# A new order table for the steps of the attention phase

## The chip, the cores and the metric

One core of a Trainium2 chip runs the whole program. The metric is the device time of one execution in microseconds (us). TensorE (PE) multiplies matrices, VectorE (DVE), ScalarE (ACT) and GpSimd (POOL) work on elements, and SyncE (SP) issues every DMA. Each engine takes its own instructions in the order in which they stand in its list; engines wait for each other through semaphores.

## The reference

Attention with a block-causal mask over 4 batches of 8 heads, 576 positions and 64 dimensions, then two mixers, all in f32 (weights of the mixers come as 64-bit floats):

```python
scores = scale * np.matmul(q, k.transpose(0, 1, 3, 2))
scores = np.where(block_i >= block_j, scores, -1000000000.0)   # blocks of 64 positions
scores = scores - np.max(scores, axis=-1, keepdims=True)
attn = np.exp(scores)
attn = attn / (np.sum(attn, axis=-1, keepdims=True) + 1e-09)
x = np.matmul(attn, v)                                         # then heads side by side: B x S x 512
u = x + (np.maximum(x.transpose(0, 2, 1) @ w_tok1, 0.0) @ w_tok2).transpose(0, 2, 1)
x = u + np.maximum(u @ w_ch1, 0.0) @ w_ch2                     # 512 -> 1536 -> 512
xn = (x - mu) / np.sqrt(var + 1e-06) * g_ln
out = x + np.maximum(xn @ w_ch1b, 0.0) @ w_ch2b                # 512 -> 2048 -> 512
```

## The kernel before

Precision is kept by splitting every operand into a high and a low part and multiplying three of the four pairs. The program has two phases.

The attention phase works on 16 pairs of heads (p = 0 to 15), eight chunks of token mixing (q = 0 to 7, two pairs each), the rebasing of the 64-bit token weights, and the first weights and rows of the MLPs. Each of these is cut into small steps, and a table of words, `ORDER`, says in which order the steps are issued. A word is a step's name and the number of its pair, chunk or tile (without a number: how often the name has come so far). There is no scheduler behind it: walking through the table fills each engine's list, so two steps of one engine run in the table's order, and a step that waits holds up all that stands behind it on that engine.

The steps of one pair, with their engines: `lqk`, `lv`, `lt` load queries and keys, values, and the last 64 positions (SP). `rlk`, `rlq` relay them (ACT, POOL). `trk`, `trq`, `trr` transpose them (PE, line 110); `kh`, `qh`, `rmh` write their high planes (ACT, line 313), `kl`, `ql`, `rml` the low ones (DVE, line 311). `s3`, `s1`, `s02`, `s4` are four groups of score matmuls (PE, lines 340, 345, 370); `m3` and so on their row maxima (DVE, lines 380, 382); `n` the negation (ACT, line 390); `e` the exponents (ACT, lines 396, 405); `h` and `l` the high and low halves of the exponents (line 425 and 429: `h3`, `h02`, `h4`, `l3`, `l1`, `l4` on POOL, `h1`, `l02` on DVE; for pair 15 `l4` is on DVE and `h1` on POOL). `tA` and `tB` are DMA transposes of those halves (SP, line 437). `a3`, `a1`, `a20`, `a4` multiply with the values (PE, lines 456, 471), whose planes are `vh` (ACT) and `vl` (DVE, line 326). `dn`, `ev`, `ev4` divide and empty the result (DVE, lines 487 and 494; ACT).

The buffers bound how far steps can run ahead: scores have two PSUM buffers, so a score group waits for the exponents of the group two before it; attention outputs have one, which `ev` (line 494) frees; three PSUM buffers serve everything else; `hlB` and `ptB`, the source and the target of `tB`, exist once, `hlA` and `ptA` twice; raw queries and keys once.

A token weight is loaded by `tl`, and rebased by `td0` (ACT), `td1` (DVE, four instructions, lines 133 to 139), `td2` (ACT), `td3` (POOL). A chunk is mixed by `xh`, `xl`, `t1a`, `t1b` (PE, line 553), `rh`, `rl`, `t2a` to `t2c` (PE, line 576), `ua` to `uc` (DVE, line 586), and stored by `us0`, `us1`. For the MLPs, `bwl` loads a weight, `bw0` to `bw3` rebase and split it (`bw1`: DVE, four instructions, lines 789 to 796), `bnl` loads a row tile (SP, line 867), `ba`, `bk`, `bh`, `bo`, `bt` scale, split and transpose it (`bo`: DVE, line 892), `b1` is the first layer of the first unit (PE, line 954).

Behind the table `Mlps.run` works through 35 units of an MLP's two layers (lines 954 and 991), with its own code and its own order.

Of the kernel before, what the change touches and what calls it, by code (L numbers as in the profile page):

```python
# [52 lines left out]
    td3:2 rlk trk td1 qh n02 kh h1 rlq e02 trr a3 trq td2:3 vl vh ql m3 tB s02 kl a20 a1 n3 s1 m02 rmh a4
    e3 vl n02 h02 l1 h4 trk rml m1 e02 td0:7 s3 lqk l02 n1 e1 td0:4 m3 tl l4 h1 rlq lv:4 s4 td0 h3 ev4 n3
    lv:3 ev m4 qh rlk n4 s1 abv ql e3 td1:4 td3:3 cmm l3 tA td1 td1 e4 abv h02 l1 tB kh kl lv m1 td2:4 n1
    s4 td2:5 abv td2 a20 l02 bwl dn a3 a1 trr tA a4 e1 s02 rmh h4 td2 m4 l4 ev s3 h1 cd1 cmm:5 h3 tB trk
    n4 ev4 rml m02 a3 l1 e4 s1 trq vh l3 a4 dn s4 m3 n02 td3:7 a1 vl e02 td3:5 h02 kh cd1:5 tA a20 cmm:4
    s02 trr:6 m1 n3 kl e3 lqk l02 h4 n1 l4 m4 xh e1 lv qh n4 h1 xl ev4 td3:4 rlq cd1:4 e4 ql trr:5 s3 vh
    rlk t1a l1 t1b vh s1 bwl:2 m02 n02 dn tB h3 vl:5 rmh:6 trq m3 ev trk h4 e02 vl:4 rmh:5 l3 bw0 n3 lqk
    rml:6 s02 dn a1 e3 rh kh m1 rlk abv rml:5 lv:8 h02 td3 a3 lv:7 rl t2b qh l4 a20 m02 l02 n1 a4 abv:8 kl  # L60
    ql ub e1 n02 tA ev t2c h3 abv:7 s4 m4 ev4 e02 cmm:8 tB uc h1 a3 trk s1 l3 rlq n4 cmm lqk l1 t2a cd1:8
    m1 xh kh cmm:6 kl s3 xl a4 n1 e4 e1 a1 h02 ua trq cd1 cd1:6 vh s02 rlq m3 vl t1a h1 a20 l02 n3 tA h4
    m02 s4 qh rlk t1b lqk e3 trq m4 ql ev4 trr n02 e02 lv vh:8 l4 n4 rh s1 e4 qh dn a1 s3 h3 rlk ev m1 l1
    rlq l3 rmh trk rl n1 trr ql rml h02 tB a3 s02 t2a e1 dn kh m3 kl rmh a4 n3 a20 vh:7 m02 l02 tA e3 lqk
    s3 rml t2c ua trq s4 m3 t2b uc m4 h4 n02 e02 trk l4 abv a1 ev4 h1 ub n3 h3 l3 qh ev bwl:1 e3 kh vl:8
    us1 us0 l1 rlq rlk s02 xh h3 n4 ql trr tB vl:7 e4 xl rmh m02 s4 trk a3 a20 m4 n02 a4 s1 h4 rml t1a e02
    kl tA n4 t1b lqk lv dn h02 trq l4 lv l3 s3 m1 n1 l02 e4 e1 kh ev rh abv kl cmm rl t2c h1 s1 ev4 l1 qh
# [1070 lines left out]
```

## Time and profile before

| | us |
|---|---|
| median of three runs | 938.29 |
| the three runs | 933.63, 938.29, 939.14 |
| the profiled execution, its own time | 932.9 |
| its span, first to last instruction | 931.1 |

| engine, over the span | busy us | instructions |
|---|---|---|
| PE | 873.0 | 5924 |
| PE weight loads | 498.5 | 5924 |
| DVE | 630.8 | 1249 |
| ACT | 346.9 | 847 |
| POOL | 215.4 | 187 |

A row of a window has its length, then busy us (and the number of instructions) of PE, PE weight loads, DVE, ACT and POOL, then the mean granted clock, the DMA share and GB/s. The shares of the whole span are an average over two phases with different limits, so stretches are read apart. In rows in order of time the first number is the start, the second the duration; brackets at a row's end give how long the engine was idle before it and what ended that. A granted clock of 1.00 is 2.4 GHz at TensorE, 0.50 is 1.2 GHz; an average between them is part of the time at either.

### The profile page before, as it was taken

What the parts mean: (1) busy time and instruction counts of PE and PEld (TensorE: products, weight loads), DVE (VectorE), ACT (ScalarE), POOL (GpSimd) and SP (SyncE); (2) the same over time, 40 slices, a digit from 0 to 9 for tenths busy, and PEclk for the clock granted to TensorE, in tenths of its full rate; (3) what the DMA queues carried; (4) which work ended last, traced back from release to release, by engine and by line L of the source; (5) the groups of instructions that cost most, each with busy time, mean ns of one, the idle gap of its engine ahead of it and who ended that gap; (6) DMA issues with size and microseconds to landing.
All of it is one profiled execution on the core that took longest, in us unless ns stands there. A gap on an engine that the chain in (4) does not pass through costs nothing.

```text
span 931.1 us, 15114 instructions
## 1 busy us (share of the span) xinstructions
PE 873.0 (94%) x5924; PEld 498.5 (54%) x5924; DVE 630.8 (68%) x1249; ACT 346.9 (37%) x847; POOL 215.4 (23%) x187
## 2 busy tenths in 40 slices
PE   6768889897889999999999989999999999999998
PEld 4657777786744454445444534455444544454444
DVE  7998889799984987678657888756555553332222
ACT  6868778886564232222212202222211221111110
POOL 4769778777000000000003434000000000000000
PEclk9679999999899999999999999999999999999999
DMA  9979999999994732221203335212011000000112
GB/s 217 223 160 207 196 206 221 180 190 196 257 235 114 202 92 91 68 68 69 68 23 69 69 90 98 93 36 68 23 46 46 23 0 1 1 1 12 57 57 79
DMA packets 193479, 96.66 MB, mean 104 GB/s; under 512 B 167744, under 2 KB 180800, under 8 KB 193408
## 3 DMA queue, kind: packets, MB, share of 16 engines
...
q14 instruction: 25, 0.20, 0.1%
...
## 4 chain that ended last, share of the span: by engine, by line
PE 43%; issue 31%; POOL 3%; DVE 2%; DMA 1%; ACT 0%; POOLq 0%
PE psy L991 21%; PE mm L954 20%; DMA ptB<-hlB 1%; POOL pl L939 1%; POOL pl L938 1%; PE mm L553 0%; POOL hlB L425 0%; POOL hlA L425 0%; POOL vr L920 0%; POOL hlB L429 0%; DVE z L931 0%; PE ps L340 0%; DVE mx L382 0%; PE mm L819 0%; DVE hlB L429 0%
## 5 line engine op out<-in xcount | busy, mean ns | idle before, releaser
L954 PE MATMUL mm<-xt,w 128*128 128x512 f16 (+1 forms) x1680 | 333.6, 358 | 4.3 <-DVE pl L892 2.9
L991 PE MATMUL psy<-w,hid 128*128 128x512 f16 x1512 | 333.8, 380 | 0.0
L954 PEld LDWEIGHTS <-w 128*128 128x128 f16 x1680 | 164.0, 98 | 167.4 <-issue 5.1
L991 PEld LDWEIGHTS <-hid 128*128 128x128 f16 x1512 | 148.2, 98 | 176.8 <-issue 1.6
L965 ACT ACTIVATE hid<-mm 128x512 f16<-128x512 f32 (+1 forms) x140 | 76.9, 552 | 381.3 <-PE mm L954 381.2
L968 DVE SCALAR_TENSOR_TENSOR hid<-mm,hid 128x512 f16<-128x512 f32 (+1 forms) x140 | 87.7, 634 | 125.0 <-ACT hid L965 125.0
L995 DVE SCALAR_TENSOR_TENSOR acc<-psy,rg,acc 128x512 f32<-128x512 f32 x72 | 53.9, 750 | 87.6 <-PE psy L991 87.6
L920 POOL TENSOR_TENSOR vr<-va,mhalf 128x4 f32<-128x4 f32 (+1 forms) x5 | 4.8, 960 | 295.8 <-DVE va L919 295.8
L340 PE MATMUL ps<-kt 64*128 64x256 f32 (+3 forms) x384 | 54.2, 400 | 18.1 <-ACT wide L405 15.2
L405 ACT ACTIVATE wide<-ps,nm 128x128 f32<-128x128 f32 (+3 forms) x128 | 65.7, 523 | 1.6
L429 POOL TENSOR_TENSOR hlA<-wide,hlA 128x1024 f16<-128x1024 f32 (+1 forms) x32 | 58.3, 1831 | 23.5 <-DVE hlA L425 15.5
L779 ACT ACTIVATE w64a<-w 128x512 f32<-128x512 f32 x56 | 37.0, 668 | 71.0 <-DVE w L859 47.7
L382 DVE TENSOR_REDUCE mx<-ps 128x2 f32<-128x768 f32 (+3 forms) x64 | 50.5, 811 | 10.7 <-PE ps L345 10.7
L995 DVE SCALAR_TENSOR_TENSOR acc<-psy,rs,acc 128x512 f32<-128x512 f32 x54 | 40.0, 748 | 26.2 <-PE psy L991 25.1
L340 PEld LDWEIGHTS ps<-kt 64*128 64x128 f32 x384 | 35.8, 223 | 26.7 <-ACT wide L405 18.9
L796 DVE SCALAR_TENSOR_TENSOR w64a<-w,w64a 128x512 int32<-128x512 int32 x56 | 40.4, 722 | 1.9
L794 DVE SCALAR_TENSOR_TENSOR w64a<-w,w64a 128x512 int32<-128x512 int32 x56 | 39.4, 703 | 1.9
L553 PE MATMUL mm<-xr,wt 128*128 128x256 f32 (+1 forms) x240 | 37.6, 307 | 0.4 <-DVE kt L311 0.4
L789 DVE TENSOR_SCALAR_CACHE_REDUCE w64a<-w64a 128x512 f32<-128x512 f32 x56 | 37.8, 674 | 0.2
L576 PE MATMUL mm<-h,wt 128*128 128x256 f32 (+1 forms) x240 | 33.1, 288 | 2.0 <-DVE kt L311 0.7
L110 PE MATMUL ptr<-ident,sc 128*128 128x128 f32 x128 | 24.0, 323 | 11.7 <-DVE kt L311 6.1
L553 PEld LDWEIGHTS mm<-xr,wt 128*128 128x128 f32 (+1 forms) x240 | 32.7, 203 | 3.7 <-PE x L471 0.5
(128 smaller groups left out, 934.5 us busy)
## 6 DMA issues: line engine op xcount, KB each, us to landing
...
```

Of the source, the lines that this page charges most:

```text
L340: nc.tensor.matmul(views[hh], kt[r, a, KQ + t * P : KQ + (t + 1) * P], kt[r, c, KK : KK + n], start=i == 0, stop=False)
L382: nc.vector.tensor_reduce(s["mx"][:, c : c + 2], ps, axis=AX.X, op=ALU.max)
L405: nc.scalar.activation(d[:, g, sl], s["ps", key][:, g, sl], AF.Exp, scale=SCALE, bias=s["nm"][:, c + g : c + g + 1], accum_out=s["rs"][:, ...
L429: (nc.vector if last else on("l" + key)).tensor_tensor(lo_, src, hi, ALU.subtract)
L553: nc.tensor.matmul(s["ps1"][:, m], w1[:r, t, a, m * P : (m + 1) * P], s["xr"][:r, c, t], start=i == 0, stop=i == 3 * NT - 1)
L794: nc.vector.scalar_tensor_tensor(ai, raw[:, :, 1], -0x40000000, ai, ALU.bitwise_and, ALU.bitwise_or)
L796: nc.vector.scalar_tensor_tensor(ai, raw[:, :, 0], 29, ai, ALU.logical_shift_right, ALU.bitwise_or)
L954: self.nc.tensor.matmul(ps.rearrange("p (t n) -> p t n", n=P), W[:, a, h * P : (h + 1) * P], self.xt[b][:, :, 4 * c + k], start=i == 0, st ...
L965: self.nc.scalar.activation(hid[:, 0, :w], ps, AF.Relu)
L968: self.nc.vector.scalar_tensor_tensor(hid[:, 1, :w], ps, 0.0, hid[:, 0, :w], ALU.max, ALU.subtract)
L991: self.nc.tensor.matmul(y, self.hid[v, h][:, a, k * P : (k + 1) * P], W[:, c], start=i == 0, stop=i == 11)
L995: self.nc.vector.scalar_tensor_tensor(self.acc[j], y, self.ps["r", v][k], self.acc[j], ALU.mult, ALU.add)
```

## The change

Only the table `ORDER` is different. It was made anew, over several sets of step durations and several phases of TensorE's clock, where the table before was made over one. Every word of the old table is in the new one, at another place; nothing else in the program differs. Its first and last rows:

```diff
 ORDER = """
-    lqk rlk tl:1 lv rlq tl:0 trk td0:1 lt td1:1 tl lqk trq kh qh td0:0 kl tl:6 tl:3 ql rlq abv s3 s1 td0
...
-    bk bs bs:8 bs
+    lqk tl:1 rlk tl:6 rlq trk td0:1 lv lv:2 td0:6 td1:1 kh trq qh lqk tl:0 kl td2:1 ql s3 m3 abv lt s1 m1
...
+    bwl bs
 """
```

VectorE, about a fifth into the attention phase, before: the last instruction of one rebase of a token weight (lines 133 to 139), two whole rebases, then a low plane of keys and, as the last row, the maximum `m1` of pair 3.

```order
L139 SCALAR_TENSOR_TENSOR w64a<-w_488,w64a 64x256
L133 TENSOR_SCALAR w64a<-w64a 128x512
L135 TENSOR_SCALAR w64a<-w64a 128x512
L137 SCALAR_TENSOR_TENSOR w64a<-w_426,w64a 128x512
L139 SCALAR_TENSOR_TENSOR w64a<-w_426,w64a 128x512
L133 TENSOR_SCALAR w64a<-w64a 128x64
L135 TENSOR_SCALAR w64a<-w64a 128x64
L137 SCALAR_TENSOR_TENSOR w64a<-w_698,w64a 128x64
L139 SCALAR_TENSOR_TENSOR w64a<-w_698,w64a 128x64
L311 TENSOR_TENSOR kt<-ptr,kt 128x512
L382 TENSOR_REDUCE mx<-ps 128x2
```

The same place after (the first rebase lacks its first instruction here); the maximum `m1` of pair 3 is the row behind two rebases:

```order
L135 TENSOR_SCALAR w64a<-w64a 128x512
L137 SCALAR_TENSOR_TENSOR w64a<-w_483,w64a 128x512
L139 SCALAR_TENSOR_TENSOR w64a<-w_483,w64a 128x512
L133 TENSOR_SCALAR w64a<-w64a 64x256
L135 TENSOR_SCALAR w64a<-w64a 64x256
L137 SCALAR_TENSOR_TENSOR w64a<-w_412,w64a 64x256
L139 SCALAR_TENSOR_TENSOR w64a<-w_412,w64a 64x256
L382 TENSOR_REDUCE mx<-ps 128x2
L429 TENSOR_TENSOR hlB<-wide,hlB 128x1024
L311 TENSOR_TENSOR kt<-ptr,kt 128x512
L380 TENSOR_REDUCE mx<-ps 128x1
```

One rebase (the 128x64 one) and the low plane of keys have moved behind this maximum; two rebases still stand ahead of it.

SyncE, near the end of the attention phase, before: from `tA` of pair 14 (first row) to `tB` of pair 15 (last row).

```order
L437 DMA_TRANSPOSE ptA<-hlA 128x24x128
L867 DMA acc_3998<-u_dram 128x512
L437 DMA_TRANSPOSE ptB<-hlB 128x26x128
L867 DMA acc_4029<-u_dram 128x512
L598 DMA u_dram<-u 64x256
L867 DMA acc_4051<-u_dram 128x512
L867 DMA acc_4085<-u_dram 128x512
L115 DMA w_4118<-in_moe_w_ch_dram 128x1024
L437 DMA_TRANSPOSE ptA<-hlA 128x24x128
L437 DMA_TRANSPOSE ptB<-hlB 128x26x128
```

And after, from the last row loads ahead of `tA` of pair 14 to `tB` of pair 15:

```order
L115 DMA w_3937<-in_moe_w_ch_dram 128x1024
L867 DMA acc_3940<-u_dram 128x512
L867 DMA acc_3967<-u_dram 128x512
L867 DMA acc_4013<-u_dram 128x512
L437 DMA_TRANSPOSE ptA<-hlA 128x24x128
L437 DMA_TRANSPOSE ptB<-hlB 128x26x128
L437 DMA_TRANSPOSE ptA<-hlA 128x24x128
L598 DMA u_dram<-u 64x256
L437 DMA_TRANSPOSE ptB<-hlB 128x26x128
```

The row loads (line 867) and the weight load (line 115) stand ahead of both transposes of pair 14; between `tB` of pair 14 and `tA` of pair 15 nothing is left, and one store (line 598) stands ahead of the last `tB`.

VectorE at the same time, before: a set of row scales, a weight rebase (line 789 to 796), two low planes of rows (line 892), and `ev` of pair 14 (line 494). Ahead of these rows stand another rebase and the two instructions of line 429 of pair 15.

```order
L826 TENSOR_SCALAR a4t<-nrm 128x4
L827 TENSOR_SCALAR a4i<-a4t 128x4
L829 TENSOR_SCALAR a4s<-a4t 128x4
L831 TENSOR_SCALAR a4i<-a4i 128x4
L832 TENSOR_SCALAR a4s<-a4s 128x4
L789 TENSOR_SCALAR w64a,mx_3267<-w64a 128x512
L792 TENSOR_SCALAR w64a<-w64a 128x512
L794 SCALAR_TENSOR_TENSOR w64a<-w_4118,w64a 128x512
L796 SCALAR_TENSOR_TENSOR w64a<-w_4118,w64a 128x512
L892 SCALAR_TENSOR_TENSOR pl<-acc_3998,a4s,pl 128x512
L892 SCALAR_TENSOR_TENSOR pl<-acc_4051,a4s,pl 128x512
L494 TENSOR_TENSOR x<-xps,den 128x4x128
```

And after, from those two instructions of line 429 on:

```order
L429 TENSOR_TENSOR hlB<-p_1_131,hlB 128x640
L429 TENSOR_TENSOR hlB<-wide,hlB 128x1024
L789 TENSOR_SCALAR w64a,mx_3307<-w64a 128x512
L792 TENSOR_SCALAR w64a<-w64a 128x512
L794 SCALAR_TENSOR_TENSOR w64a<-w_1174,w64a 128x512
L796 SCALAR_TENSOR_TENSOR w64a<-w_1174,w64a 128x512
L494 TENSOR_TENSOR x<-xps,den 128x4x128
L789 TENSOR_SCALAR w64a,mx_3307<-w64a 128x512
```

One rebase, where there were two, and no low plane of rows is left between pair 15's halves and `ev` of pair 14.

## Rows read from the trace of the kernel before

**Rows 1.** Line 954: durations in ns (min/median/max), first and last start in us.

```profile
L954 PE MATMUL mm<-xt,w x1680: 272/379/380, 262.1 to 911.7; 128*128 128x512 f16 x150, 128*128 128x256 f16 x37
```

**Rows 2.** Windows before and behind that start: busy us by engine, clock, DMA.

```profile
0.00:262.10 262.10, 214.81 (x2706) 182.40 (x2706) 228.74 (x410) 194.15 (x575) 176.06 (x146) 0.91 1.00 207
262.10:931.10 669.00, 658.18 (x3218) 316.07 (x3218) 402.06 (x839) 152.71 (x274) 39.38 (x41) 1.00 0.23 63
```

**Rows 3.** Windows of 25 us of the attention phase, same columns.

```profile
0.00:25.00 25.00, 16.27 (x79) 11.63 (x81) 18.41 (x47) 16.23 (x47) 12.13 (x22) 0.93 0.98 223
25.00:50.00 25.00, 18.29 (x186) 14.28 (x184) 22.75 (x35) 20.52 (x64) 19.47 (x17) 0.73 1.12 213
50.00:75.00 25.00, 17.02 (x247) 14.71 (x249) 22.96 (x41) 17.20 (x53) 16.61 (x12) 0.73 0.82 169
...
225.00:250.00 25.00, 18.66 (x287) 17.31 (x285) 23.69 (x56) 15.00 (x39) 5.74 (x6) 0.86 1.04 222
```

**Rows 4.** Order of time, 34 to 66 us, around the first place.

```profile
53.40 1.01 PE L340 MATMUL ps<-kt 64*128 64x256 f32 x6 [5.46 <-ACT wide L405]
...
57.12 1.39 DVE L133 TENSOR_SCALAR w64a<-w64a 128x64 f32<-128x64 f32 x1
...
59.81 0.23 DVE L139 SCALAR_TENSOR_TENSOR w64a<-w,w64a 128x64 int32<-128x64 int32 x1
...
61.27 0.29 ACT L390 ACTIVATE nm<-mx,lnp 128x2 f32<-128x2 f32 x1 [5.70 <-DVE mx L382]
...
64.27 1.33 PE L340 MATMUL ps<-kt 64*128 64x384 f32 x6 [2.92 <-ACT wide L405]
```

**Rows 5.** Order of time, 224 to 250 us, SyncE and those around it.

```profile
225.99 4.48 SPq L437 DMA_TRANSPOSE ptB<-hlB  x1
...
232.32 1.04 POOL L425 TENSOR_SCALAR hlB<-wide 128x1024 f16<-128x1024 f32 x1 [3.14 <-DMA ptB<-hlB]
...
232.85 0.37 SPq L115 DMA_DIRECT2D w<-in_moe_w_ch_dram  x1
233.32 5.58 SPq L437 DMA_TRANSPOSE ptA<-hlA  x1
...
235.05 0.81 DVE L429 TENSOR_TENSOR hlB<-p,hlB 128x640 f16<-128x640 f32 x1
...
237.69 0.69 DVE L796 SCALAR_TENSOR_TENSOR w64a<-w,w64a 128x512 int32<-128x512 int32 x1
...
239.06 4.66 SPq L437 DMA_TRANSPOSE ptB<-hlB  x1
...
243.41 0.68 DVE L494 TENSOR_TENSOR x<-xps,den 128x512 f32<-128x512 f32 x1
...
244.14 2.08 PE L456 MATMUL xps<-vt,ptA 128*128 128x64 f16 x36 [3.04 <-DVE x L494]
...
247.20 0.66 PE L471 MATMUL x<-vt,ptB 128*64 128x64 f16 x30
```

**Rows 6.** Order of time, 0 to 25 us, the tail loads and first maxima.

```profile
5.35 1.29 SPq L240 DMA_DIRECT2D qtail<-in_q_dram  x2
...
10.41 1.81 DVE L382 TENSOR_REDUCE mx<-ps 128x2 f32<-128x1024 f32 x2
...
10.91 0.47 PE L110 MATMUL ptr<-ident,qtail 128*128 128x128 f32 x1
...
12.83 0.47 ACT L390 ACTIVATE nm<-mx,lnp 128x2 f32<-128x2 f32 x2
```

**Rows 7.** Lines 429 and 326 on VectorE: busy, mean ns; then min/median/max.

```profile
L429 DVE TENSOR_TENSOR hlB<-wide,hlB 128x1024 f16<-128x1024 f32 x16 | 28.1, 1757 | 1.1 <-POOL hlB L425 1.0
...
L326 DVE SCALAR_TENSOR_TENSOR vt<-rawv,sv,vt 128x640 f16<-128x640 f32 x16 | 22.3, 1393 | 0.6 <-ACT vt L322 0.6
...
L429 DVE TENSOR_TENSOR hlB<-wide,hlB x16: 1205/1535/4278, 29.9 to 233.8; 128x1024 f16<-128x1024 f32 x16
...
L326 DVE SCALAR_TENSOR_TENSOR vt<-rawv,sv,vt x16: 869/1084/2821, 27.1 to 218.3; 128x640 f16<-128x640 f32 x16
```

More of the change, by code (lines that the diff above doesn't have):

```diff
@@ L53 @@
[L53 to L67, printed above, removed]
@@ new lines @@
+    e02 rmh m3 td2:0 rlk tl abv:1 s1 n3 m1 tA kh trq e3 cmm:2 h02 rml vl kl n1 cmm:1 h4 e1 td2:6 rml rlq
+    tl:4 td2 lqk l02 cd1 s4 s02 dn l4 cd1 qh h3 td2:2 m4 ql td0 vh n4 h1 td3:6 rlk m02 trk trr e4 l3 tl
+    trq n02 e02 td1 s3 s02 vl kh a3 tB m3 l1 dn kl m02 h02 vh rlq rmh n3 rml qh a1 e3 ql n02 s1 a4 l02 tA
+    lv m1 a20 s3 vl h4 trk s4 ev lqk td3 m3 td0:7 s1 lv e02 l4 m4 n1 h3 l3 e1 ev4 trq td0:4 n3 s4 tB e3 lv
+    kh n4 a20 td1:7 td1:4 m1 rlq rlk e4 lqk td2:7 abv:4 h02 a4 h4 l02 abv:3 n1 qh abv trr kl cmm e1 td2:4
@@ new lines @@
+    m4 l4 rmh n4 s02 e4 ql h1:3 s3 trk ev4 td3:0 cd1 rml a1 h1:2 vh a3 m02 cmm h3 m3 td3 trq tl vl bwl td0
+    bwl:2 s1 n02 tB cd1 ev e02 s02 n3 l1 a20 e3 m1 kh td1 kl qh tA ql xh l1 l3 rlq cmm n1 a4 rlk dn h02
+    trr h4 e1 td3:3 a3 trr xl rmh lv cd1 trk tA m02 l4 s4 rml t1a ev4 bwl:1 a1 vh s3 n02 lqk abv l02 m4
+    e02 h3 h1 n4 rmh ev vh l3 td2:8 cmm rml e4 tB l1 m3 cd1 n3 vl:5 t1b td2:5 s1 trq td3:7 tA td3:5 kh td3
+    a3 s02 rh kl rl m1 e3 a1 h02 h4 n1 dn m02 lv:8 qh ql e1 rlq a4 s4 rlk a20 vh vl:4 ev4 ev t2c t2b l4 s1
@@ new lines @@
+    n02 m4 l02 s3 lqk m1 h1 a1 e02 n4 uc trq e4 abv:8 h3 m3 ub l3 n1 l1 lv:7 xh t2a s02 e1 cmm:8 n3 a3 qh
+    e3 trk ua ql m02 cd1:8 vl abv:7 n02 xl tB s4 h02 dn vh:8 rlk rlq t1a l02 e02 h4 tA h1 a4 t1b a20 kh m4
+    l4 trk kl s1 cmm:7 ev4 bw0:2 n4 rh lqk e4 trq s3 trr s02 ev a3 rl m1 kh lv cd1:7 trr t2b n1 tB qh e1
+    rmh kl m3 dn rlk rml n3 vh:7 ql s4 h1 h3 l3 a4 e3 rmh vl l1 m02 ub trk tA rlq abv h4 rml lqk n02 a20
+    s3 h02 t2c us1 a1 cmm h3 lv e02 s1 m4 kh l4 ev4 n4 l3 l02 rlq m3 t2a kl ev dn l1 s02 e4 vl trq s4 n3
@@ new lines @@
+    a1 s3 xl a1 rlq e02 n1 ev m3 s02 vh lv trq s4 kl vl m02 vl h02 tB trr e1 h4 n3 dn:10 e3 bw0:0 t1a l4
+    ev4 tA dn:9 qh rlk ql a20 m4 rmh l02 us0 rml n02 e02 a4 h1 t1b abv n4 cmm a3 e4 ev h3 ev4 rh rl s3 m3
+    s02 m02 lv trk t2a xh trq t2c us0 kh cd1 l1 n3 e3 l3 qh kl trr vh ua a1 t2b n02 ql vl lqk dn s1:13
+    m1:13 tB s1:12 uc e02 xl h3 tA h4 a4 h02 a3 a20 n1:13 l4 m1:12 ub l02 rlk e1:13 s4 lv ev n1:12 rlq
+    e1:12 rmh ev4 m4 rml tB a3 s3 n4 bw1 l3 h1 h1 l1 e4 trk m3 t1a kh abv:14 s02 cmm:14 kl abv:13 n3 lqk
@@ new lines @@
+    t1b cd1:14 h4 a4 us1 a20 trq e3 rh lv h02 m02 n02 l4 s4 a1 rl t2b dn cmm:13 ev4 l02 vh:14 ev t2a rlq
+    qh ql vl:14 abv trr ub e02 cd1:13 ua rlk trq s1 l1 tA xh h3 l3 qh cmm trk rmh m4 n4 vh:13 cd1 s3 t2c
+    m1 e4 tB vh a1 rml ql xl vl:13 n1 tA e1 m3 h02 uc h4 a20 kh a4 l4 s02 n3 l02 e3 kl trr bw0:1 h3 m02
+    us0 a3 s4 n02 us1:4 e02 rmh vl l3 ev t1a ev4 us0 m4 bw1:2 n4 bwl:5 t1b tB s3 e4 a3 dn bw0:5 h1 s1 rh
+    m3 a1 bnl a4 h02 us1:3 l1 n3 rl bwl:3 h4 bnl m1 a20 bnl:3 t2a rml e3 ba:1 dn l4 l02 s02 ua bnl:2 n1 ev
```

42 lines of the change are left out of this document (16 added, 26 removed).

## The prediction

> **What bounds the kernel now.** I read where the MLPs begin first, then the two stretches that this makes, then stretches of 25 us, then the order of time where TensorE is idle. TensorE's first matmul of the channel MLPs (line 954) starts at 262.1 us [rows 1]. That instant cuts the span of 931.1 us in two [rows 2]; the execution's own time is 932.9 us, 1.8 us more. Behind it TensorE is busy for 658.18 of 669.00 us, at a granted clock of 1.00: that part is bound by matmuls, the change leaves its code alone, and I take its length as it is. Ahead of it lies the attention phase, where no engine is full: TensorE is busy for 214.81 of 262.10 us, VectorE for 228.74, ScalarE for 194.15, GpSimd for 176.06. So the phase ends when the last of a web of short chains ends, and only 262 of the 931 us can move. VectorE, the fullest, has 33.4 us idle (262.10 - 228.74); TensorE has 47.3 us. Those idle times are all that a new order can win, unless instructions themselves become shorter.
>
> The 25-us stretches [rows 3] tell where to look. In the first three TensorE is busy for 16.27, 18.29 and 17.02 us, and its granted clock averages 0.93, 0.73 and 0.73, so part of the time it runs at 1.2 instead of 2.4 GHz. From 225 to 250 us it is busy for 18.66 us. That is 6.3 us idle, a second place to look at.
>
> **The change.** Both tables hold the same 1135 words, each step exactly once, so no work is added or removed: every term below is a wait.
>
> *First place, near 51 to 64 us.* Step m1 of pair 3 (the row maxima of its second score group) stands on VectorE behind three weight-rebasing steps, twelve instructions, the last of which ends at 60.04 us (59.81 + 0.23) [rows 4]. Behind m1 waits ScalarE's negation (line 390), idle for 5.70 us; behind its exponents waits the score matmul at 64.27 us, idle for 2.92 us. An earlier score matmul, at 53.40 us, had waited 5.46 us: the exponents that free its buffer had another pair's negation ahead of them on ScalarE, and that waited for a maximum too. The new table puts the third rebase (57.12 to 60.04 us, so 2.92 us) and one 128x512 plane step (line 311) behind m1, and puts pair 3's first exponents right behind their negation. Most the two TensorE waits can give is 2.92 + 5.46 = 8.4 us; least is nothing, because VectorE is busy for 45.71 us of 25 to 75 us (22.75 + 22.96) [rows 3] and the step that is moved still has to run: the 4.3 us that it was idle there is what can be won on that engine. I take -2.5 us, somewhat more than half of these 4.3, as the waits on this engine are spread over the whole stretch.
>
> *Second place, 226 to 248 us.* Count from the start of the transpose of pair 14's second half (tB, issued by SyncE at 225.99 us) [rows 5]. SyncE needs 4.48 us for it, then issues three row loads, a store and a weight load (230.47 to 233.22 us), and only then pair 15's first transpose, at 233.32 us, which holds the queue for 5.58 us. The last transpose of all follows at 239.06 us, +13.07 us. In the new SyncE queue these five stand ahead of both transposes, and tA of pair 15 follows tB of pair 14 at once: 4.48, then 5.58, then one store, for which I put 0.6 us with the gaps (the weight load took 0.37): the last transpose can start at +10.7 us. Its data is no later: the buffer comes free at 232.32 us (+6.3), and VectorE's last of the four instructions that fill it ends at 235.86 us (235.05 + 0.81), which is +9.9 us. TensorE's last attention matmuls wait for that transpose and for VectorE: at 243.41 us line 494 empties the one PSUM buffer of attention outputs, behind two rebases and two plane steps, and TensorE idles for 3.04 us until 244.14 us. In the new order one rebase stands ahead of line 494, so it can run at about +13 us instead of +17.4 (9.9, and one rebase of 2.5: the next after 235.86 us ends at 238.38, 237.69 + 0.69). The transpose that starts at 225.99 us lets its buffer's next instruction go at 232.32 us, 6.3 us later, so the last matmuls can begin at 10.7 + 6.3 = +17.0 us. Now the last transpose lands at about 245.4 us (239.06 + 6.3) and those matmuls end at 247.86 us (247.20 + 0.66), +21.9 us: 2.5 us from landing to end. In the new order that gives +17.0 + 2.5 = +19.5 us, which is -2.4 us. VectorE, however, is nearly full here too (23.69 of 25 us [rows 3]), and in the new queue pair 14's own two transposes follow each other at once, so the first of these two can hold up the second. Range: -3.0 (the whole wait of 3.04 us) to 0, and up to +2 if pair 14's second transpose is late. I take -2.4, as every step of the chain is in the rows.
>
> *Start of the program.* The loads of the query and key tails (step lt) are put behind one more value load and the next pair's loads. Before, SyncE had made its first ten issues by 6.64 us (5.35 + 1.29), 0.66 us each, with these loads the last three, and the matmul that needs them ran at 10.91 us without a wait [rows 6]. Six more issues ahead of them are 4.0 us, so that matmul can be up to 4.0 us later. Against it, ScalarE's first negation, at 12.83 us, loses the steps that stood ahead of it, worth at most 1.5 us (12.83 - 10.41, less half of the 1.81 us that its two maxima take). I take 0, between -1.5 and +4.0.
>
> *The rest of the phase.* Counted in the two tables, 192 other VectorE steps stand between the 64 score groups and their maxima before, 182 after; five or more stand there 11 times before, 15 times after; rebases 7 times in both. That is no clear gain. I take 0, and for the bound 5 us either way, the size of one wait like that at 53.40 us (5.46).
>
> Sum: -2.5 - 2.4 = -4.9 us. Against the execution shown that gives 932.9 - 4.9 = 928.0 us. But that execution is faster than all three timed runs (933.63, 938.29, 939.14). The mean of the four is 936.0, and 936.0 - 4.9 = **931.1 us**, against a median of 938.29.
>
> **A rule that speaks against it.** Two kinds of VectorE instruction take very different times for one shape: line 429 takes 1205 ns at best, 1757 ns on average, line 326 takes 869 and 1393 ns [rows 7]. Together that is (552 + 524) ns x 16 = 17.2 us above their best. An order is laid out with some duration for each step, and a step whose duration depends on what stands beside it can be right in no such list.
> The Trainium skill, "SBUF", section "Who interferes with whom", says that a VectorE instruction with two SBUF inputs contends with a GpSimd instruction that reads SBUF, and that whichever comes first holds the shared port for its whole length. Both lines have two SBUF inputs, and the spread agrees. By the rows' means the sum stays at -4.9 us; by that rule it is open by whatever the new neighbours make of the 17.2 us, which is the slower rival below.
>
> **The rivals.**
> *The gaps only move on.* VectorE is busy for 228.74 of 262.10 us [rows 2], so a wait taken from one maximum comes back at the next rebase. For it: 15 maxima with five or more steps ahead of them after, 11 before. Against it: at the second place the chain runs through a queue, not VectorE. Time: 936.0 us.
>
> *The clock stays up.* If TensorE is fed evenly in the first 75 us, its time at the lower level goes: 16.27 x 0.07 + 18.29 x 0.27 + 17.02 x 0.27 = 10.6 us [rows 3]. For it: 0.73 lies exactly where the first place's waits are. Against it: TensorE still waits there for other engines, so not all of it counts. With three quarters, 8 us: 931.1 - 8 = 923.1 us.
>
> *Slower: VectorE's long instructions grow.* If the new order sets lines 429 and 326 beside GpSimd's long ones more often, VectorE, the fullest engine, carries it into the end of the phase. Twice the 17.2 us costs 17.2 more, half as much again 8.6; the middle is 12.9: 936.0 + 12.9 = 949 us. It decides once that growth passes the 4.9 us won. For it: line 429 has taken up to 4278 ns. Against it: GpSimd's 176.06 us are the same work in both, spread over the same phase.
>
> *The table has no effect* is ruled out: the queues differ from the first rows.
>
> **How the numbers follow.** Chances: my forecast 0.40 (its own range 925 to 937 us), gaps move on 0.22, the clock 0.18, slower 0.20. One per cent of 938.29 is 9.4 us, about what a measurement of this kernel can tell from no change (its three runs lie 5.5 us apart). Faster by over 1% means below 928.9 us: all of the clock's case and 0.15 of mine, 0.33. Slower by over 1% means above 947.7 us: 0.16 of the slower case's 0.20. The rest, 0.51, is within 1%. The range 919 to 947 us leaves out the far part of the clock's case (0.04) and the slower one above it (0.16).
>
> **What would show it.** The first matmul of line 954 should start near 257.2 us, with the stretch from it to the end still about 669 us; if that stretch moves by over 3 us, I was wrong to leave it out. First place right: no wait of over 3 us of line 390 for line 382 between 45 and 70 us. Second: the last two tB issues lie about 10.7 us apart, not 13.07, and no wait of 3 us for line 494. If line 954 starts earlier while both waits are still there, the gain came from elsewhere. The clock's case shows as 0.9 or more in 25 to 75 us; the slower one as means of over 2.0 us at line 429. My forecast is wrong if VectorE is again idle for 33 us and the phase again ends at 262 us.

## The result: 930.1 us, one per cent less

| | before | after |
|---|---|---|
| median, us | 938.71 | 930.14 |
| runs, us | 933.63, 938.29, 939.14, 940.80 | 927.36, 930.05, 930.23 |
| profiled execution, own time | 932.9 | 927.36 |
| its span | 931.1 | 925.5 |

The ratio is 0.9896, with a 95% interval of 0.9856 to 0.9936. (A fourth execution of the new kernel, of 1277 us, was disturbed and is left out.) A second measurement, eleven executions beside other kernels, gave 0.9922 (0.9888 to 0.9956). So the change is worth some 7 to 10 us, the two intervals together leave 4 to 14; the two profiled executions show 5.6 of them.

Where the phases part, in the changed kernel: line 954 (columns as in [rows 1]), the two windows that this makes (as in [rows 2]).

```profile
L954 PE MATMUL mm<-xt,w x1680: 272/379/389, 259.2 to 906.1; 128*128 128x512 f16 x150, 128*128 128x256 f16 x37
...
0.00:259.10 259.10, 211.06 (x2706) 179.78 (x2706) 225.17 (x409) 196.70 (x576) 170.76 (x146) 0.90 1.01 209
259.10:925.50 666.40, 658.43 (x3218) 316.02 (x3218) 402.80 (x841) 152.80 (x272) 39.38 (x41) 1.00 0.23 64
```

The attention phase ends 3.0 us sooner (262.1 to 259.1 us), the stretch behind it is 2.6 us shorter (669.00 to 666.40). In the profile of the second measurement (after_again) line 954 starts at 263.7 us and 665.8 us lie behind it: the earlier end of the phase is not repeated, the shorter stretch is. VectorE is idle for 33.9 us ahead of the cut, as long as before (33.4).

The tail, which was the prediction's second place, in order of time on SyncE, as in [rows 5]:

```profile
227.15 3.96 SPq L437 DMA_TRANSPOSE ptB<-hlB  x1
231.20 3.61 SPq L437 DMA_TRANSPOSE ptA<-hlA  x1
234.91 0.54 SPq L598 DMA_DIRECT2D u_dram<-u  x1
236.93 3.89 SPq L437 DMA_TRANSPOSE ptB<-hlB  x1
```

From `tB` of pair 14 to `tB` of pair 15 it is now 9.78 us instead of 13.07. But the first of these two starts 1.2 us later than before.

The first place: `m1` of pair 3 in order of time on VectorE, as in [rows 4]; it starts at 51.39 us, 60.55 before. In the second execution of the same kernel it starts at 56.54 us (last two rows).

```profile
51.05 0.42 DVE L139 SCALAR_TENSOR_TENSOR w64a<-w,w64a 64x256 int32<-64x256 int32 x1
51.39 0.67 DVE L382 TENSOR_REDUCE mx<-ps 128x2 f32<-128x512 f32 x1
...
55.77 0.84 DVE L139 SCALAR_TENSOR_TENSOR w64a<-w,w64a 64x256 int32<-64x256 int32 x1
56.54 0.67 DVE L382 TENSOR_REDUCE mx<-ps 128x2 f32<-128x512 f32 x1
```

There is also a stall that the kernel before did not have. ScalarE stands 5.26 us at 184 us, in the exponents `e1` of pair 12, until GpSimd frees their buffer. Order of time, GpSimd and then ScalarE; behind it the windows of TensorE around it:

```profile
177.19 0.72 POOL L425 TENSOR_SCALAR hlB<-p 128x640 f16<-128x640 f32 x1 [3.08 <-DMA ptB<-hlB]
...
181.82 2.12 POOL L429 TENSOR_TENSOR hlA<-wide,hlA 128x1024 f16<-128x1024 f32 x1
...
183.97 0.47 ACT L405 ACTIVATE wide<-ps,nm 128x256 f32<-128x256 f32 x1 [5.26 <-POOL hlA L429]
...
180.00:185.00 5.00, 1.15 (x27) 0.87 (x25) 2.64 (x3) 1.03 (x5) 3.93 (x3) 0.90 0.76 150
185.00:190.00 5.00, 4.96 (x24) 4.29 (x24) 4.66 (x10) 3.95 (x12) 1.41 (x2) 0.50 0.95 235
```

The step that frees the buffer, `l3` of pair 12 (at 181.82 us), had nothing to wait for itself. It stands in GpSimd's list behind `h4`, `h02`, `l4` of pair 11, and `h4` waited until 177.19 us for the transpose `tB` of pair 10. TensorE then does 1.15 us of work in 5, and in the next 5 its granted clock is 0.50, that is 1.2 GHz.

### The profile page after: what moved, and what is told of

The parts are those of the page before. It is cut to its first block, busy times and chain, and to the rows that moved or that the text cites. A ratio compares the mean times of both kernels' runs of the same rounds, so it can differ in the third digit from the quotient of the medians.

```text
span 925.5 us, 15107 instructions
## 1 busy us (share of the span) xinstructions
PE 869.5 (94%) x5924; PEld 495.8 (54%) x5924; DVE 628.0 (68%) x1249; ACT 349.5 (38%) x847; POOL 210.1 (23%) x187
## 4 chain that ended last, share of the span: by engine, by line
PE 42%; issue 30%; POOL 3%; DVE 2%; DMA 1%; POOLq 0%; ACT 0%
PE psy L991 21%; PE mm L954 20%; POOL pl L939 1%; POOL pl L938 1%; DMA ptB<-hlB 1%; DMA w<-in_moe_w_ch_dram 1%; POOL vr L920 0%; DVE z L931 0%; POOL hlB L429 0%; DVE vt L326 0%; PE ps L340 0%; POOL hlB L425 0%; PE mm L819 0%; DVE mx L382 0%; POOL hlA L429 0%
## 5 line engine op out<-in xcount | busy, mean ns | idle before, releaser
L405 ACT ACTIVATE wide<-ps,nm 128x256 f32<-128x256 f32 (+3 forms) x128 | 65.8, 523 | 11.5 <-POOL hlA L429 9.8
L340 PE MATMUL ps<-kt 64*128 64x256 f32 (+3 forms) x384 | 52.1, 384 | 12.6 <-ACT wide L405 10.3
L429 POOL TENSOR_TENSOR hlA<-wide,hlA 128x1024 f16<-128x1024 f32 (+1 forms) x32 | 55.3, 1735 | 11.7 <-DVE hlA L425 11.0
L576 PEld LDWEIGHTS mm<-h,wt 128*128 128x128 f32 (+1 forms) x240 | 30.4, 187 | 5.0 <-issue 2.6
```

Source lines behind the costliest of these rows:

```text
L340: nc.tensor.matmul(views[hh], kt[r, a, KQ + t * P : KQ + (t + 1) * P], kt[r, c, KK : KK + n], start=i == 0, stop=False)
L405: nc.scalar.activation(d[:, g, sl], s["ps", key][:, g, sl], AF.Exp, scale=SCALE, bias=s["nm"][:, c + g : c + g + 1], accum_out=s["rs"][:, ...
L429: (nc.vector if last else on("l" + key)).tensor_tensor(lo_, src, hi, ALU.subtract)
L576: nc.tensor.matmul(ps[:r, k], w2[:, m, a, t * P : t * P + r], s["h1"][:, c, m], start=i == 0, stop=i == 5)
```

## The experiments

All of them reorder the same 1135 steps. BEFORE and AFTER below are the two tables as lists of steps; a mixture takes the first steps of one and then all that is left in the order of the other. At a join, 4 to 13 steps stand elsewhere than in either table, which is a small change of its own that no run here separates. The kernel before was run beside every series (86 undisturbed executions: mean 936.7 us, standard deviation 3.2).

**Is it the first place?** Once everything around it alone, once the changed kernel with it undone.

```diff
-ORDER = BEFORE
+ORDER = AFTER[:260] + rest of BEFORE
```

> The first 260 steps in the new order (they hold m1:3 and all that was moved around it), the rest as in the kernel before. Two readings are to be told apart. Gains carry: the 9.2 us by which m1:3 starts sooner (51.39 us after, 60.55 before) are partly kept, the load tB:14 starts 2 to 6 us sooner than the 225.99 us of before, the first matmul of L954 stands at 256 to 260 us instead of 262.1, and the median is 2 to 6 us under the kernel before. Gaps only move on: the lead of 7.5 us at tB:2 is gone by the loads of pairs 6 to 8, L954 stands within 1 us of 262.1, and the median is within 1.5 us of the kernel before.

Measured: 1.0005 (0.9976 to 1.0035). `m1` of pair 3 starts at 51.76 us, as in the changed kernel. TensorE's first matmul of line 954 in the profiled execution starts at 259.6 us; the stretch behind it is 672.7 us. So line 954 came 2.5 us sooner in the execution shown, which is no more than such starts differ between executions of one kernel (259.1 and 263.7 us above), and the time of the kernel shows no gain.

```diff
 # pairs 3, 4 and token weight 8, AFTER
-m1 ... kl ... tl:8 ... td0:8 ... td1:8
+tl:8 ... td0:8 td1:8 kl m1
```

> The changed kernel with the order at the first place put back: td1:8 and kl:4 (and tl:8 and td0:8, which td1:8 needs) run ahead of m1:3 again. Theory of the prediction: PE meets the waits of 5.46 and 2.92 us of before again, m1:3 starts 3 to 9 us later than the 51.39 us of the changed kernel, and the median is 2 to 3 us above the changed kernel (932 to 933 us). Rival, that m1:3 comes sooner for another reason (the clock and all the steps before it): m1:3 starts within 2 us of 51.39, and the median is within 1 us of the changed kernel.

Measured: 0.9897 (0.9859 to 0.9936), the ratio of the changed kernel. Order of time on VectorE, and TensorE's waits between 40 and 66 us (waiting line <- line waited for: us in total, times, longest):

```profile
55.82 1.46 DVE L139 SCALAR_TENSOR_TENSOR w64a<-w,w64a 128x64 int32<-128x64 int32 x1
57.20 0.68 DVE L311 TENSOR_TENSOR kt<-ptr,kt 128x512 fp32r<-128x512 f32 x1
57.80 0.68 DVE L382 TENSOR_REDUCE mx<-ps 128x2 f32<-128x512 f32 x1
...
PE pt L256 <- DVE kt L311: 2.8, 1, 2.8
PE ps L340 <- ACT wide L405: 2.5, 2, 2.1
PE ptr L110 <- DVE kt L311: 1.5, 1, 1.5
```

`m1` stands behind the rebase and the plane step again. Counted from the end of the 64x256 rebase that runs ahead of it in all three executions, it starts 3.8 us later (53.97 to 57.80 us), where it follows at once in both executions of the changed kernel (51.47 to 51.39 and 56.61 to 56.54). So the local reading was right: these steps do hold it up. But TensorE's waits of 5.46 and 2.92 us do not come back. It has 7.2 us of waits there, the longest 2.8. That lies between the 6.0 and 9.3 us of the two executions of the changed kernel (9.2 in the kernel before), so the waits tell no difference, and nothing of the move is seen in the time of the program.

**Is it the second place, the tail?**

```diff
-ORDER = BEFORE
+ORDER = BEFORE[:890] + rest of AFTER
```

> The order of the kernel before for the first 890 steps, the new order for the rest (the second place of the prediction, and the last steps before the MLP). Theory: the load tB:14 starts at 226.0 us as before, tB:15 9.8 to 10.7 us later instead of 13.07, the first matmul of L954 stands at 258.5 to 260 us, and the MLP stretch is 666.4 us as in the changed kernel if its 2.6 us come from what runs last before it: median 2.5 to 5 us under the kernel before. Rival: the three and a half us won at the end belong to the lag of 1.2 us at tB:14 that is only made good there; then L954 stands at 261 to 262 us and the median is within 1.5 us of the kernel before.

Measured: 0.9985 (0.9960 to 1.0010), 936.29 us; the execution with the profile was the slowest of the twelve (943.71 us), so its 276.2 us for line 954 says nothing. The distances in it do: 665.7 us from line 954 to the end (666.4 foreseen), `tB` of pair 14 to that of pair 15 9.8 us as foreseen, but `tB` of pair 13 to that of pair 14 19.2 us instead of 12.5.

**Which part holds the gain?** Both tables have nearly the same set of steps ahead of step 424 (about 95 us) and ahead of step 762 (about 180 us), so they were cut there.

```diff
-ORDER = BEFORE
+ORDER = AFTER[:424] + rest of BEFORE                                      # y3_A424
+ORDER = (BEFORE[:424], then AFTER up to 762) + rest of BEFORE             # y2_mid
+ORDER = BEFORE[:762] + rest of AFTER                                      # y4_late
+ORDER = AFTER[:762] + rest of BEFORE                                      # y1_A762
+ORDER = (AFTER[:424], then BEFORE up to 762) + rest of AFTER              # z_nomid
+ORDER = AFTER                                                             # after_again
```

> The kernel before up to step 424, the new order from there to the new order's step 762 (pairs 5 to 11, some 95 to 182 us), and the order of before for the rest. Neither place of the prediction is in it. Theory after the first runs: the gain sits in this middle, where the load tB:7 starts 12.3 us after tB:6 in the changed kernel and 17.5 us in the kernel before; then tB:6 to tB:7 is 11.5 to 12.5 us here too, L954 stands 3 to 7 us sooner than 262.1, and the median is 4 to 9 us under the kernel before. Rival, that the gain is made of parts that help only together (a head that is ahead of the loads, and a tail that starts the MLP sooner): the median is within 2 us of the kernel before.

> The new order up to step 762, just ahead of the stall at 178 to 185 us, and the order of before for the rest. Theory: the lead of about 7 us that the changed kernel has at 180 us is kept to the end, since the stall of 5.26 us at e1:12 is not there: L954 stands at 254 to 257 us; the start of the MLP is that of before (a stretch of 669 to 673 us, with PE's wait for pl of L892 of about 3 us), so that the median is 5 to 9 us under the kernel before. Rival: the lead is lost in any order of the last quarter, since what comes last waits for the DMA queue and not for PE's lead: L954 within 2 us of 262.1, median within 2 us of the kernel before.

> The new order up to step 424 (some 95 us, the head of the first runs and pairs 3 to 5 on top), the order of before for the rest. Theory that the gain sits in the middle behind it: a median within 2 us of the kernel before, and the load tB:7 again 16.9 to 17.5 us after tB:6. Rival, that the lead of 60 matmuls (4.6 us) which the changed kernel has at 100 us is kept: L954 at 257 to 259 us, median 3 to 6 us under the kernel before.

> The changed kernel once more, unchanged, beside the others on one chip: what its median and its L954 are worth as a yardstick. A median of 0.985 to 0.994 of the kernel before; L954 between 256 and 264 us in the profile, since the phase ahead of it differs by some us from one execution to the next (259.1 in the first profile; 263.6 with the first place undone at an equal median); the stretch behind L954 665 to 667 us, the stall of ACT at e1:12 of 4 to 6 us seen again.

> The new order up to step 424 and from step 762 on, the order of before in the middle between them. The middle alone was 1.003 of the kernel before, and yet the new order up to 762 was 2.7 us under it while the one up to 424 was 1.9 us over it. Theory, that the middle helps only with the head and the last quarter of the same order around it: the median is 3 to 5 us above the changed kernel (933 to 936 us). Rival, that the middle is worth nothing and all of the gain sits in the last quarter: the median is within 1.5 us of the changed kernel (929 to 932 us).

> The order of before up to step 762, the new order for the last quarter (with the stall of ACT at e1:12, the closer loads at the tail and the seam to the MLP). Theory, that most of the gain is the seam (3 to 4 us) and the tail loads, less 4.3 us of the stall: the stretch from tB:15 to the end 687.6 to 688.6 us, tB:14 to tB:15 9.8 us, and the median 2 to 5 us under the kernel before. Rival, that the last quarter holds the whole gain: 7 to 9 us under the kernel before (929 to 931). Other rival, that the stall eats it all: within 1.5 us of the kernel before.

| to 424 | 424 to 762 | from 762 | ratio to before | 95% interval |
|---|---|---|---|---|
| new | old | old | 1.0020 | 0.9977 to 1.0062 |
| old | new | old | 1.0030 | 0.9997 to 1.0064 |
| old | old | new | 0.9991 | 0.9965 to 1.0017 |
| new | new | old | 0.9971 | 0.9937 to 1.0006 |
| new | old | new | 0.9973 | 0.9943 to 1.0002 |
| new | new | new | 0.9922 | 0.9888 to 0.9956 |

No part alone is faster beyond its interval. The three alone add up to +0.0041 (0.0020 + 0.0030 - 0.0009), with a 95% half width of 0.0060 (the root of the sum of the squared half widths); the whole is -0.0078, with one of 0.0034. The difference, 0.0119, is beyond both together (0.0069). So these three do not add up to the whole: the theory that the gain sits in the middle fell with y2_mid, and the one that the last quarter holds it fell with y4_late. Two of the three parts together, in the two pairs that were tried, bring a third of it, and their intervals reach 1. z_nomid, at 933.14 us, lies where its theory had it (933 to 936), and after_again came out as expected: line 954 at 263.7 us, 665.8 us behind it, a stall of 4.7 us.

But the three have four joins between them. Cut once only, at step 762, the halves (0.9971 and 0.9991) add up to -0.0038 (half width 0.0043). That is 0.0040 from the second measurement of the whole, within both together (0.0055), and 0.0066 from the first, just beyond (0.0059). The other sum with four joins, z_nomid and y2_mid, is 0.0081 off. A cost of 2 to 3 us at each join, an estimate from these differences, would do as well as parts that need each other. No run tells the two apart.

Where the time goes between fixed points can be read off SyncE's queue, by the starts of the transposes `tB` (6 is pair 6; all us, profiled executions):

| | tB 6 | 6 to end | 6 to 7 | 11 to 12 | 13 to 14 | 14 to 15 | 15 to end |
|---|---|---|---|---|---|---|---|
| before | 119.8 | 811.3 | 17.5 | 12.2 | 12.5 | 13.1 | 692.0 |
| x1_head | 118.2 | 814.1 | 17.4 | 12.4 | 12.5 | 13.2 | 695.4 |
| y3_A424 | 122.4 | 815.5 | 17.5 | 13.2 | 13.5 | 13.0 | 694.1 |
| y2_mid | 126.3 | 812.7 | 12.2 | 13.2 | 14.2 | 12.8 | 693.8 |
| y1_A762 | 122.2 | 809.6 | 12.2 | 12.2 | 12.1 | 13.3 | 694.3 |
| y4_late | 122.8 | 813.1 | 17.5 | 16.8 | 16.9 | 10.5 | 688.9 |
| z_nomid | 121.1 | 811.4 | 17.5 | 16.4 | 16.3 | 10.5 | 688.0 |
| after | 117.6 | 807.9 | 12.3 | 17.6 | 16.8 | 9.8 | 688.6 |
| after_again | 122.7 | 806.8 | 11.8 | 17.6 | 16.9 | 10.4 | 687.6 |
| x3_undo_first | 120.2 | 808.5 | 11.6 | 17.9 | 16.8 | 9.8 | 688.1 |
| x5_l3 (below) | 118.3 | 803.0 | 11.6 | 12.7 | 15.6 | 9.8 | 688.3 |

Four things repeat in every execution of the table with the new last quarter: 14 to 15 is shorter by about 3 us and 15 to end by 3 to 8 us (the seam to the MLPs), but 13 to 14 is longer (15.6 to 16.9 us for 12.1 to 14.2) and, x5_l3 apart, 11 to 12 by 3 to 6 us. That they nearly cancel fits y4_late. In the three executions with the new middle as well, 11 to 12 holds the stall at 184 us; in y4_late and z_nomid it does not, though the expectation of y4_late put it there: ScalarE's wait for GpSimd's line 429 is 1.9 us in both, not 5, and what makes 11 to 12 long in them was not found.

The new middle has one such mark too: 6 to 7 takes 11.6 to 12.3 us in all executions with it, 17.4 to 17.5 with the old one. So the 5 us that y2_mid was to win are there, as its theory said, and yet the kernel is no faster: 6 to 11 is 66.5 us in it for 69.3 before, and 13 to 14 is 1.7 us longer. In y1_A762 line 954 starts at 260.5 us, not at 254 to 257: there, too, a lead was not kept.

`tB` of pair 6 has the same place in both tables (step 503 and 502), so its start can be compared: it is 117.6 and 122.7 us in two executions of the same changed kernel. A difference of 3 us ahead of it cannot be read from one profile of each.

**The seam alone.** In the kernel before, the profile puts TensorE's first longer wait in line 954 down to VectorE's line 892. ScalarE stood in a norm (`ba`, line 874) that waits for its row's load, with `bh` (line 887) behind it, and VectorE waited for `bh`. Rows of the kernel before, ScalarE and VectorE in order of time, and TensorE's wait (columns as for the waits above):

```profile
266.38 0.63 ACT L874 ACTIVATE njunk<-acc 128x512 bf16<-128x512 f32 x1 [2.41 <-DMA acc<-u_dram]
...
267.01 0.71 ACT L887 ACTIVATE pl<-acc,a4s 128x512 f16<-128x512 f32 x1
...
267.75 0.75 DVE L892 SCALAR_TENSOR_TENSOR pl<-acc,a4s,pl 128x512 f16<-128x512 f32 x1 [2.58 <-ACT pl L887]
...
PE mm L954 <- DVE pl L892: 2.9, 1, 2.9
```

```diff
 # ScalarE and VectorE, BEFORE
-bh:6 ba:8 bh:7 bh:5 ba:10 bh:4 ... uc:7 ... bo:5 ... bo:4
+bh:6 bh:5 bh:4 ba:8 bh:7 ba:10 ... bo:5 bo:4 uc:7
```

> The kernel before with one thing of the new order alone, at the seam to the MLP: bh:4 and bh:5 (ACT, L887) run ahead of the norms ba:8 and ba:10 (ACT, L874), and bo:4 and bo:5 (DVE, L892) ahead of uc:7. In the kernel before ACT stood 2.41 us in ba:10 for the load of its row, with bh:4 behind it; DVE waited 2.58 us for bh:4 and PE 2.9 us for DVE. Theory: these waits go, the stretch from the load tB:15 to the end is 688 to 690 us (692.0 to 695.4 in five executions with this part as before, 687.6 to 688.6 with the new one), and the median is 2.5 to 4.5 us under the kernel before. Rival: PE's time there is only moved, since the rows that come next (L892 of the other batches, the transposes bt) are as late as before; then the stretch is 691 to 695 us and the median within 1.5 us of the kernel before.

Measured: 0.9997 (0.9968 to 1.0025), and from `tB` of pair 15 to the end 693.1 us: no gain, with a wait of 2.54 us at the same matmul. The order of time of TensorE and SyncE shows why. Before:

```profile
262.15 10.52 PE L954 MATMUL mm<-xt,w 128*128 128x512 f16 x48 [0.24 <-DMA xt<-pl]
...
266.25 7.02 SPq L902 DMA_TRANSPOSE xt<-pl  x3
...
275.53 7.93 PE L954 MATMUL mm<-xt,w 128*128 128x512 f16 x36 [2.86 <-DVE pl L892]
```

With the seam edit:

```profile
265.26 10.52 PE L954 MATMUL mm<-xt,w 128*128 128x512 f16 x48
...
269.29 6.86 SPq L902 DMA_TRANSPOSE xt<-pl  x3
...
278.32 9.62 PE L954 MATMUL mm<-xt,w 128*128 128x512 f16 x36 [2.54 <-DVE mhalf L767]
```

And in the changed kernel:

```profile
259.15 10.52 PE L954 MATMUL mm<-xt,w 128*128 128x512 f16 x48 [1.52 <-DMA xt<-pl]
...
264.99 3.59 SPq L902 DMA_TRANSPOSE xt<-pl  x2
...
270.46 10.53 PE L954 MATMUL mm<-xt,w 128*128 128x512 f16 x48 [0.79 <-DMA xt<-pl]
```

TensorE does 48 matmuls on the first four rows and then stops, for the second four. What the profile names for this is a VectorE instruction that ended about then, a plane of a later row or a memset, neither of which these matmuls read; the planes of the second four rows were done by 268.50 us (267.75 + 0.75) in the kernel before. What fits all three is the last transpose `bt` of those rows on SyncE (line 902): it is issued by 273.27, 276.15 and 268.58 us, and line 954 goes on 2.26, 2.17 and 1.88 us later. The edit brought the planes forward, not the transposes, which stand behind the stores of chunk 7 and take SyncE as long as before (6.86 and 7.02 us for three). In the new order the last is issued 9.4 us after line 954 begins, before it was 11.1. So the theory took the releaser by its name in the profile and moved the wrong step.

An earlier `bt` alone was not tried, but the fourteen profiled executions of the study agree. In the six with the old end of the table that last transpose is issued 10.9 to 11.9 us after TensorE's first matmul of line 954, and TensorE stops for 2.5 to 3.5 us. In four with the new end it is 8.8 to 9.6 us, and the stop 0.2 to 1.0 us. In the other four it is 8.2 to 8.4 us, and TensorE runs on without a stop. Wherever it stops, it goes on 1.9 to 2.3 us after that issue.

**The stall at 184 us.** The one experiment on a cause that the profile of the changed kernel names.

```diff
 # GpSimd, AFTER
-h3:12 h4:11 h02:11 l4:11 rlq:14 l3:12
+h3:12 l3:12 h4:11 h02:11 l4:11 rlq:14
```

> The changed kernel with one step of POOL, l3:12 (L429), moved from behind h4:11, h02:11, l4:11 and rlq:14 to right behind h3:12. Theory: the wait of 5.26 us of ACT at 184 us (e1:12, L405, for the buffer that l3:12 frees) goes, and with it PE's waits of 2.16 and 1.74 us there; the lead of 7.6 us that the changed kernel has at tB:11 is kept in part up to tB:14 (223 to 226 us instead of 227.15), L954 stands at 255 to 258 us instead of 259.1, and the median is 1 to 4 us under the changed kernel (926 to 929). Rival: the stall there is POOL's wait for the DMA of tB:10, which moves on to the next step of POOL whatever stands there: L954 stands within 1 us of 259.1 and the median is within 1 us of the changed kernel.

Measured: 0.9883 (0.9848 to 0.9919), 926.22 us, the fastest kernel of the study. The stall is gone: `tB` 11 to 12 is 12.7 us (17.6 to 17.9 in the three executions that have it; 12.5 in the next kernel, which keeps this move). GpSimd's step in order of time, and the window of 25 us of this kernel:

```profile
174.58 2.59 POOL L429 TENSOR_TENSOR hlA<-wide,hlA 128x1024 f16<-128x1024 f32 x1
...
175.00:200.00 25.00, 20.27 (x305) 18.10 (x304) 23.82 (x40) 17.78 (x56) 19.24 (x14) 1.00 1.01 193
```

and of the changed kernel:

```profile
175.00:200.00 25.00, 19.25 (x276) 17.19 (x274) 17.91 (x29) 15.00 (x50) 15.89 (x13) 0.86 0.75 154
```

`l3` runs at 174.58 us, 7.2 us sooner. In the same 25 us TensorE does 305 instead of 276 matmuls, VectorE works 5.9 us more, and the clock stays at 1.00. From `tB` of pair 11 to the end it is 739.5 us, 743.8 to 744.0 in the three executions with the stall: 4.3 us, from one profile of this kernel. As a whole the kernel is 0.1 to 0.4% under the two measurements of the changed kernel (0.9896 and 0.9922); the intervals overlap, so that size is not shown by the times, only that the stall and the 4.3 us behind it are gone.

**The same remedy once more.** In the last kernel GpSimd still waits 6.37 us for the transpose of pair 13, with `l1` of pair 14 and so `tA` of pair 14 behind it.

```diff
 # GpSimd and SyncE, x5_l3
-tB:13 ... h1:14 ... bnl:0 h02:14 us1:3 l1:14 bwl:3 ... bnl:1 bnl:3 bnl:2 tA:14 tB:14
+tB:13 ... h1:14 l1:14 ... tA:14 bnl:0 h02:14 us1:3 bwl:3 ... bnl:1 bnl:3 bnl:2 tB:14
```

> The changed kernel with l3:12 right behind h3:12 as in x5_l3 (which ended the stall of ACT at e1:12), and the same at the next place of its kind: l1:14 (POOL, L429), which stood behind h02:14 while that waited 6.4 us for the transfer of tB:13, goes ahead of it, and the load tA:14 ahead of the loads bnl:0, us1:3 and bwl:3. Theory: tA:14 starts at 211 to 215 us where x5_l3 had 218.35, tB:14 at 220 to 222 where it had 223.25, L954 at 253 to 256 us, and the median is 1 to 3 us under x5_l3 (0.985 to 0.988 of the kernel before). Rival: PE is bound there by its own work and by the loads of pair 15: the ratio is that of x5_l3, 0.988 to 0.990.

Measured: 0.9966 (0.9935 to 0.9997), 933.88 us: 7.7 us slower than x5_l3. Order of time, GpSimd's `l1`, then SyncE, ScalarE, TensorE:

```profile
215.42 1.16 POOL L429 TENSOR_TENSOR hlA<-wide,hlA 128x512 f16<-128x512 f32 x1 [5.45 <-DVE hlA L425]
...
216.61 3.49 SPq L437 DMA_TRANSPOSE ptA<-hlA  x1
220.14 0.64 SPq L867 DMA_DIRECT2D acc<-u_dram  x1
...
221.99 2.04 SPq L867 DMA_DIRECT2D acc<-u_dram  x3
...
226.73 0.63 ACT L874 ACTIVATE njunk<-acc 128x512 bf16<-128x512 f32 x1 [8.03 <-DMA acc<-u_dram]
...
228.79 1.81 PE L370 MATMUL ps<-kt 128*128 128x288 f32 x6 [6.44 <-ACT wide L405]
```

`l1` came only 1.7 us sooner (215.42 us for 217.16 in x5_l3), since it was not ready: the half `h1` that it needs is written by VectorE, behind a weight rebase, until 215.35 us (215.29 in x5_l3). `tA` was put ahead of four row loads on SyncE. It waits there for `l1` until 216.61 us, and the loads, at 213.02 to 216.7 us in x5_l3, go out at 220.14 to 224.03 us. ScalarE has one norm of those rows in the middle of its exponents, and stands in it for 8.03 us; TensorE waits 6.44 us for the exponents behind it. `tB` of pair 15 comes 15.5 us after that of pair 14 instead of 9.8. What the move pushed back, not what it pulled forward, decided. The two moves were not tried one by one.

## Why the prediction came out right, point by point

The number (931.1 us for a measured 930.14) and the side are right; most of the way to it is not. The sum put the whole gain ahead of line 954 and none behind it. But the phase ends at 259.1 and 263.7 us in the two profiles, where 257.2 was foreseen and 262.1 was before, while the stretch behind it is shorter in both. And neither place, tried alone, shows the gain that was summed for it. That the total came out is luck.

*The base.* The execution shown of before was taken as a quick one and the mean of the four times, 936.0 us, as the base. The 86 later executions counted above have a mean of 936.7. This step held, and without it the same sum would have given 928.0.

*The first place, -2.5 us.* The mechanism is as told in part: `m1` no longer stands behind those steps, the waits of 5.46 and 2.92 us [rows 4] are no more there as they were (TensorE's longest for line 405 is 2.0 us in the first profile and 3.2 in the second), and line 390 waits for line 382 no longer than 0.5 and 2.0 us at a time between 45 and 70 us. What failed is that such a gain lasts. x1_head puts its worth at 0 (+0.5 us, give or take 2.8), which just leaves out the -2.5 us. x3_undo_first, which lacks it, is level with the first measurement of the changed kernel and 2 us under the second; give or take 5 us, that alone decides nothing.

*The second place, -2.4 us.* The distance came out at 9.78 us for 10.7 foreseen and TensorE has no wait of 3 us for line 494 (0.8 us in the second profile, none in the first). The caveat in the same step, that pair 14's own transposes come late, came true and was the larger part: 13 to 14 is longer by some 4 us, where +2 was allowed for. The tail alone measures -1.4 us (give or take 2.3).

*The start and the rest, 0.* At the start the matmul on the query tail came 2.5 us later (13.43 for 10.91 us) and the first negation 0.5 us sooner (12.30 for 12.83 us), both inside the range. The rest was not nothing but several things of 3 to 6 us: 6 to 7 shorter, 11 to 12 and 13 to 14 longer. They were put at nothing because the counts of steps ahead of the maxima (five or more: 11 before, 15 after) looked no better. Such a count shows none of them.

*The MLPs' stretch, unchanged.* Wrong by 2.6 us in the first pair of profiles, and not by chance: 15 to end is 687.6 to 688.9 us in all executions with the new end of the table, 692.0 to 695.4 with the old one. From line 954 on it is 665.1 to 666.4 us in the eight profiled executions with the new end and 669.0 to 672.7 in the six with the old one. The means are 5.3 us apart, more than the whole forecast of 4.9, and about half of that (2.7 us, from the means again) is the stop of TensorE described at the seam. The seam of the two phases belongs to the table, since rows, planes and transposes of the first units are steps in it.

*Gaps only move on (936.0 us).* For each place and each part alone the time is that of no change, as this rival has it. For the whole table it is not.

*The clock.* Refuted as told: 25 to 75 us has 0.62 and 0.73 in the changed kernel, not 0.9. (Its price adds up to 10.7 us, not 10.6, which changes nothing.) But the rows show more than that. Windows of 25 us of the changed kernel, two executions, first and second measurement:

```profile
0.00:25.00 25.00, 14.79 (x77) 10.42 (x78) 16.61 (x45) 16.62 (x46) 10.56 (x21) 0.90 0.99 223
25.00:50.00 25.00, 20.83 (x198) 16.50 (x196) 24.59 (x44) 22.27 (x70) 19.13 (x16) 0.62 1.08 224
50.00:75.00 25.00, 16.86 (x248) 14.48 (x247) 24.20 (x40) 18.16 (x55) 21.55 (x18) 0.73 1.02 205
```

```profile
0.00:25.00 25.00, 15.68 (x73) 10.82 (x73) 15.92 (x43) 15.87 (x43) 10.20 (x20) 1.00 0.98 232
25.00:50.00 25.00, 17.73 (x186) 13.48 (x186) 24.66 (x42) 20.52 (x66) 19.84 (x16) 1.00 0.97 209
50.00:75.00 25.00, 14.79 (x193) 12.20 (x194) 23.79 (x33) 18.33 (x55) 20.53 (x17) 0.73 0.97 199
```

The same list of instructions ran 25 to 50 us at 0.62 in one execution and at 1.00 in the other, and the one at 1.00 was not ahead for it: 452 matmuls by 75 us against 523, and 929.5 us of span against 925.5. x5_l3 and z_best, alike up to step 742 and run on a chip of the same number, had 0.93 and 0.64 there. So that clock figure in [rows 3] was a property of the execution, not of the order, and no argument could rest on it.

*Slower by longer VectorE instructions.* Refuted. Line 429 and line 326 on VectorE after, as in [rows 7]:

```profile
L429 DVE TENSOR_TENSOR hlB<-wide,hlB 128x1024 f16<-128x1024 f32 x16 | 27.2, 1699 | 2.3 <-POOL hlB L425 2.3
...
L326 DVE SCALAR_TENSOR_TENSOR vt<-rawv,sv,vt 128x640 f16<-128x640 f32 x16 | 20.3, 1270 | 0.0
```

Means of 1699 and 1270 ns for 1757 and 1393: 2.9 us less in all ((58 + 123) ns x 16); in the second execution 1624 and 1215 ns, 5.0 us less. The rule of the Trainium skill ("SBUF — State Buffer", "Who interferes with whom") stays in line with the spread; that GpSimd is its cause was not tested. The mean does not tell the time of a kernel, either: line 429 has 2008 ns in x3_undo_first and 1548 in x5_l3, both about 1% under the kernel before, so the sign set for this rival (over 2.0 us) can show without it.

**What stays open.** Why the mixtures bring less than the whole. A part laid out for one state of all queues meets another one when its neighbours are exchanged, and the joins can cost something too; no run tells these apart. Between `tB` of pair 6 and the end the changed kernel wins 3.5 to 4.5 us on the kernel before. By the table that is some 5 us at 6 to 7, 3 at 14 to 15 and 3.5 to 4.5 behind, less 5 at 11 to 12 and 4 at 13 to 14. Of these only the stall in 11 to 12 was traced to a step by an experiment. That the choice over several durations and clock phases is what made the table better was not tested either.
